# Means of v copied by engines instead of DMAs, and the first up products in parts by head group

## The chip, the cores and the metric

The kernel runs on one core of one Trainium2 chip. The metric is the device time of one execution in microseconds; each kernel is run several times and the median counts. A profile is one more execution, with its own time.

## The reference

Four batches, eight heads, 768 positions, head dimension 64. Each query attends to the keys less than 16 positions away and, beside them, to one summary for each block of 32 keys: the maximum of the block's keys, and the mean of its values. Then a feed-forward layer follows, whose activation is h cos h.

```python
k_sum = k.reshape(B, H, nb, block, D).max(axis=3)
v_sum = v.reshape(B, H, nb, block, D).mean(axis=3)
scores_l = np.where(mask_l, scale * q @ k.T, -1e9)       # |i - j| < 16
scores_s = scale * q @ k_sum.T + np.log(block)
a = softmax(concat(scores_l, scores_s))
x = (a @ concat(v, v_sum)) -> (3072, 512)
h = x @ w_in            # 512 x 2048
out = (h * np.cos(h)) @ w_out
```

(The `@` forms are shortened here; the softmax adds 1e-9 to its sum.) The weights come as 64-bit floats.

## The kernel before, in words

The 3072 rows are eight blocks of 384, two to a batch. In each block the eight heads make four groups of two, `a` to `d`; `a0` is the first group of block 0, `c1` the third of block 1. One group's attention gives 128 of the 512 rows of x, transposed: `x_high` rounds the product to the short float that PE multiplies at full rate, `x_low` takes what is left. x of groups a and b lies in one tile, x of c and d in another.

The layer runs in *steps*: one step takes 128 of the 2048 columns of `w_in` for one block. `up` is 12 matmuls (four groups, three products of high and low parts) into one PSUM bank; `turns` (ACT), `residue` (DVE), `sine` (ACT) and `gate` (DVE) make h cos h; `high_part` and `low_part` split it; `down` and `down_low` are 9 matmuls into three accumulators. Steps s0 to s5 are block 0 with the first six weight slices, s6 to s21 block 1 with all 16, s22 to s31 block 0 with the rest; from s32 on a block is done at a time. A weight slice (`w0` to `w15`) is loaded as raw bytes into one of a few slots and made into floats by `apart` and `first_bits` (ACT), `join` (DVE), and split by `high_part` and `low_part`, the last on DVE or POOL.

Blocks 0 and 1 are done ahead of the layer's first step or beside it. A group there goes: load q and k; transpose k (`tk`, two halves) and q (`tq`) on PE into PSUM; copy them to SBUF (`ck` on ACT or DVE, `cq`); block maxima of k (`ks`, DVE); mask and score matmuls (`ms`, `sc`, PE); minimum (`mx`, DVE), exponentials (`ex`, ACT, six instructions), sums (`sm`, DVE), inverse (`iv`), multiplication (`nm`, POOL); transposes of the weights (`tp`, two pieces, PE), their copies to SBUF (`cp`); the products with the values (`va`, 24 matmuls, PE); `xh` and `xl`.

The value tile of a group has 96 rows of values and, in rows 96 to 119, the 24 block means, the same for each of its six windows. For batch 0 the means are made on PE: `Summaries.load` brings v in two halves (`v0_0.l`, `v0_1.l`, two DMAs each), `Summaries.products` (`vm`, L908) multiplies each by a matrix of 1/32 and 0, `ones`, into 24 rows of a bank; `place` (`ve`, L919) copies four pieces of that bank to four small tiles `means` with ACT; and `load_vs` (`m`, L502) lets SP send each piece to a value tile, six times over, once for each block: eight DMAs in all. The other batches have another way, which stays.

The order is written out by hand: `ORDER` (L32) is one list of tokens such as `a0.tk.1.0`, what to do, with its PSUM banks and its engine (`a`, `v`, `p` for ACT, DVE, POOL). The program walks it, and each engine's queue, SP's too, has its instructions in the order of the list. `FILL` (L22) puts filling matmuls ahead of some tokens (L960): they multiply zeros, and nothing reads them. There are 56 in twelve places.

## Time and profile before

| | us |
|---|---|
| runs shown: median (lowest to highest) | 635.62 (633.67 to 638.09) |
| profiled execution, from its first instruction to its last | 633.6 |
| PE busy in it | 620.6 (98%) |
| DVE, ACT, POOL busy | 426.8, 315.7, 208.7 |
| mean granted clock of TensorE | 1.000 |

The page lists for each engine what share of the span it was busy, then the same in 40 slices of 15.8 us as digits of tenths, and the costliest groups of instructions: line, engine, operation, tiles, shapes and count, then busy us and the mean ns of one, then the idle time of the engine ahead of them and what ended it. The other views used are: busy time of each engine by stretches of the span; the timeline, a row for each run of equal instructions with its start and length; the chain of work that ended last, in order of time; the view of waits. PEld is PE's loading of the stationary operand; SPq the queue from which the DMAs are issued. A matmul's row has its whole length, through which the next ones already run, so the time that one takes of PE is read from many in a row.

### The profile page before, as it was taken

Reading aid. Unit: us, or ns where it says so; the run is one execution under the profiler, and the core shown is the slowest. Engines: PE = TensorE matmul, PEld = TensorE weight load, DVE = VectorE, ACT = ScalarE, POOL = GpSimd, SP = SyncE. Lnnn points to the kernel's source line nnn. Section 1 sums busy time; section 2 is a strip of 40 time slices with the busy share of each in tenths; the row PEclk is TensorE's granted clock in tenths of the full one; section 3 lists DMA queues with packets and bytes.
Section 4 is the critical chain, followed back from the end, with each engine's and each line's share of the span. In section 5 each row is a group of like instructions: output and inputs, shape, how many; then the busy total and the mean of one; then the engine's idle time right before and its main releaser. Section 6 shows DMA issues by size and latency. Waiting matters only on the chain.

```text
span 633.6 us, 12128 instructions
## 1 busy us (share of the span) xinstructions
PE 620.6 (98%) x4596; PEld 546.6 (86%) x4596; DVE 426.8 (67%) x795; ACT 315.7 (50%) x557; POOL 208.7 (33%) x243
## 2 busy tenths in 40 slices
PE   7889999999999999999999999999999999999997
PEld 5469898988889989897998989898888998989895
DVE  5689889986767877766766576657775555554524
ACT  3588776765544454464534554353554352522323
POOL 3136543563532523243434432211432241201000
PEclk9999999999999999999999999999999999999999
DMA  8987876734354465434343544232242313300001
GB/s 218 289 235 203 283 238 187 164 80 109 104 157 123 100 152 117 110 87 115 77 128 98 134 109 109 72 78 62 72 116 87 100 47 98 93 25 34 17 1 50
DMA packets 171305, 74.10 MB, mean 117 GB/s; under 512 B 136944, under 2 KB 160112, under 8 KB 171248
## 3 DMA queue, kind: packets, MB, share of 16 engines
q1 hardware_dynamic: 171104, 73.21, 43.6%
q8 instruction: 36, 0.59, 0.4%
q14 instruction: 21, 0.17, 0.1%
q10 hardware_dynamic: 144, 0.13, 0.1%
HBM read 54.43 MB, written 16.52 MB: 112 GB/s over the span
## 4 chain that ended last, share of the span: by engine, by line
PE 91%; SPq 3%; DVE 2%; DMA 2%; ACT 1%; POOL 0%; issue 0%; DVEq 0%; ACTq 0%
PE banks L738 41%; PE banks L789 41%; PE banks L694 4%; PE banks L581 3%; DMA late<-in_moe_w_out_dram 2%; SPq L468 2%; PE banks L650 1%; PE banks L593 0%; ACT L756 0%; SPq L497 0%; SPq L906 0%; SPq L489 0%; ACT t L756 0%; DVE t L760 0%; DVE xl L389 0%
## 5 line engine op out<-in xcount | busy, mean ns | idle before, releaser
L738 PE MATMUL banks<-xh,w 128*128 128x384 f32 x1024 | 267.0, 337 | 0.0
L789 PE MATMUL banks<-w,gh 128*128 128x512 f32 x768 | 197.4, 392 | 0.6 <-DVE stage L827 0.6
L738 PEld LDWEIGHTS banks<-xh,w 128*128 128x128 f32 x1024 | 185.3, 188 | 2.4 <-issue 1.3
L738 PE MATMUL banks<-xl,w 128*128 128x384 f32 x512 | 171.1, 334 | 0.0
L789 PEld LDWEIGHTS banks<-w,gh 128*128 128x128 f32 x768 | 142.7, 188 | 31.4 <-issue 1.2
L389 POOL TENSOR_TENSOR gl<-t,gh 128x384 fp32r<-128x384 f32 x67 | 68.7, 1029 | 240.2 <-DVE gh L385 84.6
L748 ACT ACTIVATE t<-banks 128x384 int32<-128x384 f32 x128 | 62.3, 489 | 162.4 <-PE banks L738 88.0
L751 DVE SCALAR_TENSOR_TENSOR t<-t,banks 128x384 f32<-128x384 int32 x128 | 69.7, 547 | 66.7 <-ACT t L748 66.3
L789 PE MATMUL banks<-w,gl 128*128 128x512 f32 x384 | 108.7, 391 | 0.0
L760 DVE TENSOR_TENSOR t<-t,banks 128x384 f32<-128x384 f32 x128 | 69.6, 548 | 41.9 <-ACT t L756 40.2
L756 ACT ACTIVATE t<-t 128x384 f32<-128x384 f32 x128 | 66.3, 523 | 63.0 <-DVE t L751 62.7
L738 PEld LDWEIGHTS banks<-xl,w 128*128 128x128 f32 x512 | 96.1, 188 | 0.3
L789 PEld LDWEIGHTS banks<-w,gl 128*128 128x128 f32 x384 | 71.8, 188 | 15.3 <-issue 0.2
L641 POOL TENSOR_TENSOR sc<-sc,r 128x720 f32<-128x720 f32 x28 | 40.1, 1432 | 58.6 <-DVE r L638 54.5
L383 ACT CAST gh<-t 128x384 fp32r<-128x384 f32 x62 | 31.4, 510 | 35.3 <-DVE t L760 19.2
L617 POOL TENSOR_TENSOR sc<-sc,m 128x720 f32<-128x720 f32 x24 | 34.0, 1415 | 44.5 <-DVE m L614 41.3
L389 DVE TENSOR_TENSOR gl<-t,gh 128x384 fp32r<-128x384 f32 x61 | 38.9, 640 | 11.5 <-ACT gh L383 6.6
L385 DVE CAST gh<-t 128x384 fp32r<-128x384 f32 x66 | 25.3, 383 | 15.8 <-PE banks L789 12.5
L254 POOL TENSOR_TENSOR kn<-kn 96x256 f32<-96x256 f32 (+1 forms) x38 | 25.7, 677 | 23.7 <-DMA kn<-in_v_dram 22.0
L601 DVE SCALAR_TENSOR_TENSOR sc<-banks,mask 128x360 f32<-128x360 f32 x48 | 24.2, 519 | 13.4 <-PE banks L581 13.4
L635 DVE TENSOR_REDUCE r<-sc 128x6 f32<-128x726 f32 x28 | 25.1, 897 | 10.0 <-ACT sc L631 9.6
L664 DVE STREAM_TRANSPOSE stage<-sc 128x768 f32<-128x768 f32 x24 | 23.3, 970 | 10.5 <-POOL sc L641 10.2
(115 smaller groups left out, 558.0 us busy)
## 6 DMA issues: line engine op xcount, KB each, us to landing
pd<-stage SPq DMA_DIRECT2D x24, 384.0 KB
late<-in_moe_w_out_dram SPq DMA_DIRECT2D x16, 511.6 KB
late<-in_moe_w_in_dram SPq DMA_DIRECT2D x16, 510.5 KB
pt<-pd SPq DMA_DIRECT2D x72, 96.0 KB
vn<-in_v_dram SPq DMA_DIRECT2D x50, 120.0 KB
out_dram<-stage SPq DMA_DIRECT2D x23, 256.0 KB
kn<-in_v_dram SPq DMA_DIRECT2D x24, 192.0 KB
qn<-in_q_dram SPq DMA_DIRECT2D x96, 48.0 KB
```

The costliest lines, as they stand in the source:

```text
L254: eng.tensor_tensor(out=t[:, :n], in0=t[:, :n], in1=t[:, n:], op=ALU.add)
L383: eng.copy(out=out, in_=in_)
L389: eng.tensor_tensor(out=lo, in0=src, in1=hi.bitcast(F32), op=ALU.subtract)
L617: nc.gpsimd.tensor_tensor(out=self.sc, in0=self.sc, in1=self.m.unsqueeze(2).broadcast_to([P, U, NK]), op=ALU.subtract)
L641: nc.gpsimd.tensor_tensor(out=self.sc, in0=self.sc, in1=self.r.unsqueeze(2).broadcast_to([P, U, NK]), op=ALU.mult)
L694: nc.tensor.matmul(out=self.xps[rows, t * QT : (t + 1) * QT], lhsT=self.vn[:, t, rows], rhs=self.pt[2 * c + hh][s], start=True, stop=True,)
L738: nc.tensor.matmul(out=self.h, lhsT=w_of(name, self.f)[:, c * P : (c + 1) * P], rhs=x_of(self.blk, part, c), start=n == 0, stop=n == last,)
L748: nc.scalar.activation(out=self.t.bitcast(I32), in_=self.h, func=AF.Copy, scale=1.0 / TWO_PI, bias=0.25)
L751: nc.vector.scalar_tensor_tensor(out=self.t, in0=self.t.bitcast(I32), scalar=-TWO_PI, in1=self.h, op0=ALU.mult, op1=ALU.add)
L756: nc.scalar.activation(out=self.t, in_=self.t, func=AF.Sin, scale=-1.0, bias=-0.5 * math.pi)
L760: nc.vector.tensor_tensor(out=self.t, in0=self.t, in1=self.h, op=ALU.mult)
L789: nc.tensor.matmul(out=self.acc[i], lhsT=g[:, i * P : (i + 1) * P], rhs=w_of(name, self.f), start=self.first and n == 0, stop=self.last an ...
```

## The change

Three things.

1. `means` and `place` go. `ones` becomes wider, so that the products of v write 120 rows of the bank, the means in rows 96 to 119 and zeros above. `load_vs` for batch 0 is now an engine's copy of 24 rows and 768 columns: for block 0 from the bank (each piece read six times over), for block 1 from the value tile of the same group of block 0. The engines are ACT for a0, b0, c0, c1; DVE for d0, d1; POOL for a1, b1.
2. `up` is now made of four `up_part`, one for each head group, three matmuls each; a token `pu` calls one alone, and the first to come has the bank. Steps s0 to s5 use it; all later steps call `up` as before, with the same matmuls in the same order.
3. `ORDER` is new from its start up to `s31.tu`; the remaining two thirds of the list, 1396 tokens of 2096, are the old ones. `FILL` keeps one entry, 15 filling matmuls ahead of the first mask (`c0.ms`, now the first token); the other 41 go. In the new part many tokens have another engine: of the high parts of x of blocks 0 and 1, seven of eight are on DVE (all eight were on ACT), the low parts of w1, w0, w4, w7, w6 and w12 went from DVE to POOL and that of w5 from POOL to DVE, and the high parts of w1, w5 and w4 from DVE to ACT.

```diff
-FILL = {"a0.tk.1": 15, "a0.tk.0": 2, "b0.tq": 8, "c0.tk.0": 2, "b0.tk.0": 2, "d0.tk.0": 2, "b0.tk.1": 3, "c0.tp.0": 9, "b1.ms": 4, "b1.tq": 3, "a1.ms": 3, "a0.va": 3}
+FILL = {"c0.ms": 15}
...
-    ones = early[:, U * P : U * P + QC * 3 * HB].rearrange("p (c n) -> p c n", c=QC)
+    ones = early[:, U * P : U * P + QC * (NK + HB)].rearrange("p (c n) -> p c n", c=QC)
...
-        def load_vs(self):
+        def load_vs(self, eng=None):
             if not self.b:
-                nc.sync.dma_start(
-                    out=self.vn[W:NK], in_=means[self.pr].unsqueeze(1).broadcast_to([NB, U, P])
-                )
+                if self.half:
+                    means = groups[0][self.pr].vn[W:NK]
+                else:
+                    means = Summaries.bank[W:NK, self.pr * P : (self.pr + 1) * P].unsqueeze(1).broadcast_to([NB, U, P])
+                copy(eng, self.vn[W:NK], means)
                 return
...
         def up(self, i):
-            self.h = bank(i)[:, :TB]
-            n, last = 0, 3 * NC - 1
             for c in range(NC):
-                for name, part in (("wi_h", 0), ("wi_h", 1), ("wi_l", 0)):
-                    nc.tensor.matmul(
-                        out=self.h, lhsT=w_of(name, self.f)[:, c * P : (c + 1) * P],
-                        rhs=x_of(self.blk, part, c),
-                        start=n == 0, stop=n == last,
-                    )
-                    n += 1
+                self.up_part(c, *([] if c else [i]))
+
+        def up_part(self, c, *i):
+            if i:
+                self.h, self.n = bank(*i)[:, :TB], 0
+            for name, part in (("wi_h", 0), ("wi_h", 1), ("wi_l", 0)):
+                nc.tensor.matmul(
+                    out=self.h, lhsT=w_of(name, self.f)[:, c * P : (c + 1) * P], rhs=x_of(self.blk, part, c),
+                    start=self.n == 0, stop=self.n == 3 * NC - 1,
+                )
+                self.n += 1
...
-                Summaries.bank = bank(*i)[:NB, : H * D]
+                Summaries.bank = bank(*i)[:NK, : H * D]
...
-                    out=Summaries.bank, lhsT=ones[:, c, (1 - self.n) * HB : (3 - self.n) * HB], rhs=t[:, :, c],
+                    out=Summaries.bank, lhsT=ones[:, c, (1 - self.n) * HB :][:, :NK], rhs=t[:, :, c],
...
-        def place(self, eng):
-            for i in range(NG):
-                copy(eng, means[i], Summaries.bank[:, i * P : (i + 1) * P])
```

What the list does to the queues is seen at three places. First PE, at the place where the layer begins. Before (`pt` are the transposed weights of the attention, `early` the value tile of b0, `w_394` the slice w1):

```order
L694 MATMUL banks<-pt,early 64x64 x12
L650 MATMUL banks<-ident,sc 120x128 x6
L738 MATMUL banks<-xh_0_568,w_394 128x384
L738 MATMUL banks<-xl_0_604,w_394 128x384
L738 MATMUL banks<-xh_0_568,w_394 128x384 x2
L738 MATMUL banks<-xl_0_604,w_394 128x384
L738 MATMUL banks<-xh_0_568,w_394 128x384
L738 MATMUL banks<-xh_0_589,w_394 128x384
```

Now (`x_1_156` and `early` are the value tiles of d0 and b0, `w_500` the slice w0, `w_380` w1; `xh_0_597` is x of c and d, `xh_0_527` x of a and b):

```order
L699 MATMUL banks<-pt,x_1_156 64x64 x12
L655 MATMUL banks<-ident,sc 120x128 x4
L747 MATMUL banks<-xh_0_527,w_500 128x384
L747 MATMUL banks<-xl_0_535,w_500 128x384
L747 MATMUL banks<-xh_0_527,w_500 128x384
L747 MATMUL banks<-xh_0_597,w_500 128x384
L747 MATMUL banks<-xl_0_602,w_500 128x384
L747 MATMUL banks<-xh_0_597,w_500 128x384
L699 MATMUL banks<-pt,early 64x64 x12
L524 MATMUL banks<-ident,qn 128x128 x3
```

Before, all values of block 0 stand ahead of the first up product; now two parts of s1 are done behind the values of a0 and c0, and six more of s1 and s0 between the values of d0, of b0 and the scores of d1. The scores of d1 stood ahead of the first up product and now stand behind eight parts.

Second ACT, where the means are copied. Before (`late2` to `late5` hold the small tiles, `stage1` is a raw slice):

```order
L626 ACTIVATE late5_145<-banks_153,m_368 128x120 x6
L383 COPY pt_388<-banks_153 120x256
L383 COPY late2_142<-banks_153 24x128
L383 COPY late3_143<-banks_153 24x128
L383 COPY late4_144<-banks_153 24x128
L383 COPY late5_145<-banks_153 24x128
L417 ACTIVATE stage1_449<-late6_146 128x1024
```

Now (`early`, `vn` and `x1_0` are the value tiles of b0, a0 and c0):

```order
L631 ACTIVATE sc_122<-banks_153,m_360 128x120 x6
L386 CAST w1_380<-stage1_344 128x1024
L386 COPY early_148<-banks_153 24x768
L386 COPY vn_120<-banks_153 24x768
L386 COPY x1_0_155<-banks_153 24x768
L386 COPY pt_398<-banks_153 120x256
L386 COPY kd3_119<-banks_153 128x384 x2
L420 ACTIVATE stage1_480<-late6_146 128x1024
```

Three copies of 768 columns stand in the place of four of 128, ahead of the P^T copies and of d0's k copies.

Third SP's queue of loads, up to the second half of v (`late_140` and `late_141`). Before (`kn` is d0's k):

```order
L468 DMA kn<-in_k_dram 128x6x64 x2
L468 DMA late_142<-in_k_dram 128x6x64 x2
L906 DMA late_140<-in_v_dram 128x4x192 x2
L468 DMA late_145<-in_q_dram 128x3x64 x2
L468 DMA qn<-in_q_dram 128x3x64 x2
L404 DMA late_147<-in_moe_w_in_dram 128x4x1021
L408 DMA late_147<-in_moe_w_out_dram 128x4093
L906 DMA late_141<-in_v_dram 128x4x192 x2
```

Now:

```order
L407 DMA late_147<-in_moe_w_in_dram 128x4x1021
L411 DMA late_147<-in_moe_w_out_dram 128x4093
L471 DMA late_144<-in_q_dram 128x3x64 x2
L471 DMA qn<-in_q_dram 128x3x64 x2
L913 DMA late_140<-in_v_dram 128x4x192 x2
L913 DMA late_141<-in_v_dram 128x4x192 x2
L471 DMA kn<-in_k_dram 128x6x64 x2
```

The slice w1 stands ahead of both halves of v, the halves follow each other, and d0's k comes behind them; the eight DMAs of the means, of 72 KB each, no longer stand further down.

More of the change, by code (lines that the diff above doesn't have):

```diff
@@ L170 @@
+s127.ta.0.0.v s127.st.0 s127.ta.1.1.a s127.st.1 s127.ta.2.a s127.st.2 s127.sb.2
 """
@@ L353, in tile_kernel @@
     HB = NB // 2
-    ones = early[:, U * P : U * P + QC * 3 * HB].rearrange("p (c n) -> p c n", c=QC)
+    ones = early[:, U * P : U * P + QC * (NK + HB)].rearrange("p (c n) -> p c n", c=QC)
     nc.gpsimd.memset(ones, 0.0)
-    nc.gpsimd.memset(ones[:, :, HB : 2 * HB], 1.0 / BLOCK)
+    picks = ones[:, :, W + HB : NK]
+    nc.gpsimd.memset(picks, 1.0 / BLOCK)
     for base, sign in ((0, 1), (BLOCK - 1, -1)):
         nc.gpsimd.affine_select(
-            out=ones[:, :, HB : 2 * HB], in_=ones[:, :, HB : 2 * HB], pattern=[[sign, QC], [-sign * BLOCK, HB]],
+            out=picks, in_=picks, pattern=[[sign, QC], [-sign * BLOCK, HB]],
             compare_op=ALU.is_ge, fill=0.0, base=base, channel_multiplier=sign * QC,
@@ L871, in tile_kernel @@
     vn_b = [carve(late[3 + i // 2], i % 2 * n_v, NK, U, P) for i in range(NG)]
-    means = [carve(late[2 + i], 2 * n_v + TB, NB, P) for i in range(NG)]
     slices = [Slice(f, late[int(i)][:, :RAW]) for f, i in enumerate(SLOTS)]
@@ L940, in tile_kernel @@
         ),
-        Summaries: dict(l="load", h="halve", s="sum", vm="products", ve="place"),
+        Summaries: dict(l="load", h="halve", s="sum", vm="products"),
         Slice: dict(
@@ L946, in tile_kernel @@
         Step: dict(
-            up="up", tu="turns", re="residue", si="sine", ga="gate", hi="high_part",
+            up="up", pu="up_part", tu="turns", re="residue", si="sine", ga="gate", hi="high_part",
             lo="low_part", dh="down", dl="down_low", fe="fetch", ad="add", ta="take", st="store",
```

275 lines of the change are left out of this document (138 added, 137 removed).

## The prediction

> **What bounds the kernel now.** I read the page first: span, busy shares and the row of slices.
>
> ```profile
> span 633.6 us, 12128 instructions
> PE 620.6 (98%) x4596; PEld 546.6 (86%) x4596; DVE 426.8 (67%) x795; ACT 315.7 (50%) x557; POOL 208.7 (33%) x243
> PE   7889999999999999999999999999999999999997
> ```
>
> PE is busy for 98% of the span, and only the first three slices and the last one fall short of 9. The question is thus how much PE time is open, and where. The view of busy time by stretches tells it (PE, PEld, DVE, ACT, POOL, then granted clock, DMA share and GB/s):
>
> ```profile
> 0.00:47.50 47.50, 39.57 (x643) 27.96 (x643) 33.87 (x72) 28.62 (x71) 13.33 (x42) 1.00 0.91 247
> 47.50:160.00 112.50, 112.50 (x740) 101.58 (x739) 96.44 (x159) 76.21 (x128) 56.83 (x57) 1.00 0.64 181
> 160.00:163.00 3.00, 2.38 (x13) 1.97 (x12) 2.47 (x3) 1.63 (x3) 0.91 (x1) 1.00 0.41 134
> 163.00:600.00 437.00, 436.92 (x3063) 389.17 (x3063) 282.32 (x541) 199.81 (x338) 135.62 (x142) 1.00 0.37 93
> ```
>
> From 47.5 to 600 us PE is idle 0.7 us in all. Before 47.5 it is idle 7.9 us, and part of its busy time there is the filling matmuls of L960, which compute nothing. What stands at 47.5 is in the timeline and the chain: the first up product, and behind it four in a row.
>
> ```profile
> 47.50 0.42 PE L738 MATMUL banks<-xh,w 128*128 128x384 f32 x1
> 47.74 8.35 PE banks L738 x48
> ```
>
> So an up matmul takes 8.35/48 = 0.174 us of PE, and from the first one to the end PE is the bound. **A gain can only come from useful matmuls done before 47.5 us; a loss can come from anywhere, since behind 47.5 every wait of PE adds to the span.** The order is new up to step 31; behind that it is the old one, so I let that part run its old length.
>
> **The change, part by part.** I sum against the profiled execution, 633.6 us; the median of the three runs shown, 635.62, lies 2.0 above it, and the forecast is that sum plus 2.0.
>
> *The means.* Before, the second half of v landed late enough to hold PE; ACT then wrote four small tiles, and SP sent them to the value tiles by DMA, the last of the four only at 38.57.
>
> ```profile
> 23.42 2.73 PE L914 MATMUL banks<-late,early 128*24 128x512 f32 x6 [1.21 <-DMA late<-in_v_dram]
> 26.19 0.73 ACT L383 COPY late<-banks 24x128 f32<-24x128 f32 x4 [3.26 <-PE banks L914]
> 38.57 0.82 SPq L504 DMA_DIRECT2D early<-late  x1
> ```
>
> In the new order d0's k (two DMAs) stands behind both halves of v on SP; all other loads ahead of them are the same ones. Its size, by the rows of DMA issues:
>
> ```profile
> kn<-in_k_dram SPq DMA_DIRECT2D x2, 192.0 KB
> ```
>
> That is 0.39 MB, at the 247 GB/s of the first stretch 1.6 us. The second half of v then lands at 21.8 instead of 23.4, and its products end at 24.5. They write 120 rows instead of 24, with as many columns, so I leave them 2.73. ACT now stands still at the first mean copy (b0's) until 24.5; queued behind it are every P^T copy, k copy and score exponential of the first stretch, so **ACT's list from there is the next chain**. No copy of 24x768 is in the trace; the two sizes of ACT's P^T copy give its slope:
>
> ```profile
> L383 ACT COPY pt<-banks 120x512 f32<-120x512 f32 x4 | 2.4, 590 | 0.3 <-PE banks L650 0.2
> L383 ACT COPY pt<-banks 120x256 f32<-120x256 f32 x6 | 2.3, 382 | 1.2 <-PE banks L694 0.7 <-PE banks L650 0.5
> ```
>
> 208 ns for 256 columns makes 0.80 us for 768. The four small copies above took 0.18 us for 128 columns each, so 1.1 for six of them is the upper end; the slope alone, without the 0.17 us that an instruction of this line costs beside it, is the lower, 0.6. For the two copies on POOL the nearest rows are the clearing of a tile's edge and a subtraction:
>
> ```profile
> L877 POOL MEMSET x<- 120x128 f32 x2 | 0.3, 203 | 0.0
> L389 POOL TENSOR_TENSOR gl<-t,gh 128x384 fp32r<-128x384 f32 x67 | 68.7, 1029 | 240.2 <-DVE gh L385 84.6 <-PE banks L789 66.7 <-ACT gh L383 65.0
> ```
>
> 0.2 us, and twice 1.03 for 768 columns: between 0.2 and 2.1, middle 1.1, and hidden, since POOL is idle for over two thirds of the first stretch.
>
> *ACT's list up to the first up product's turns.* The other durations:
>
> ```profile
> L417 ACT ACTIVATE stage<-late 128x1024 f32<-128x1024 int8 x16 | 18.4, 1151 | 6.0 <-DMA late<-in_moe_w_out_dram 4.0 <-DVE w L389 1.7 <-POOL w L389 0.3
> L422 ACT ACTIVATE stage<-stage 128x1024 int32<-128x1024 f32 x16 | 16.9, 1059 | 0.3
> 29.99 1.60 ACT L626 ACTIVATE sc<-banks,m 128x120 f32<-128x120 f32 x6
> L383 ACT COPY kd<-banks 128x384 f32<-128x384 f32 x6 | 2.8, 480 | 4.6 <-PE banks L532 4.6
> L525 ACT ACTIVATE qd<-banks 128x384 f32<-128x384 f32 x2 | 1.0, 502 | 2.3 <-PE banks L519 2.3
> L383 ACT CAST w<-stage 128x1024 fp32r<-128x1024 f32 x4 | 4.2, 1047 | 1.1 <-DVE stage L429 1.1
> ```
>
> Between the wait and the first turns (`s0.tu`) the new order gives ACT: 4 mean copies 3.2; 2 k copies 0.96; 4 short and 2 long P^T copies 2.7; `apart` and `first_bits` of w0, w2, w5 6.63; 4 sets of exponentials 6.4; 3 q copies 1.5; one w cast 1.05. Sum 22.4, with 26 gaps of 0.03 us between neighbours 23.2. From 24.5 that ends at 47.7, and the q copy of d1, 0.8 us earlier, at 46.9. d1's scores follow on PE (1.0 us): **48.0 us for what PE had behind it at 47.5 before.** But by then 8 up parts (of s1 and s0), 24 matmuls, are done as well, in the gaps: 24 x 0.174 = 4.2 us. DVE comes out about even: four casts of x and a mean copy go to it, two slice casts and, net, one slice low part leave it. **Term 1: 4.2 - 0.5 = 3.7 us won.** The removed fillings are worth nothing in themselves, they lay in waits.
>
> *The next 14 us.* Further rows:
>
> ```profile
> L748 ACT ACTIVATE t<-banks 128x384 int32<-128x384 f32 x128 | 62.3, 489 | 162.4 <-PE banks L738 88.0 <-DVE gl L389 35.8 <-POOL gl L389 34.6
> L756 ACT ACTIVATE t<-t 128x384 f32<-128x384 f32 x128 | 66.3, 523 | 63.0 <-DVE t L751 62.7
> L756 ACT ACT_TABLE_LOAD x23 | 29.5, 1283 | 0.4
> L383 ACT CAST gh<-t 128x384 fp32r<-128x384 f32 x62 | 31.4, 510 | 35.3 <-DVE t L760 19.2 <-PE banks L789 14.8 <-DVE t L751 1.2
> L383 ACT CAST xh<-banks 128x384 fp32r<-128x384 f32 x23 | 10.9, 481 | 11.1 <-PE banks L694 11.1
> 36.74 0.85 PE banks L694 x24
> 37.59 0.58 PE banks L650 x4
> 93.48 8.20 PE banks L789 x36
> ```
>
> From 48.0 PE has 12 more parts (6.3 us, steps 2, 5 and 3), one set of values 0.85, one of P^T 0.58 and the down products of s0 and s1 (18 x 8.20/36 = 4.1): it reaches the down product of s2 at 59.8. That one needs s2's gate cast on ACT. ACT's list from 47.7 to there: 4 turns 2.0, 3 sines 1.6, the table load 1.3, `apart` and `first_bits` of w3 and w4 4.4, exponentials 1.6, w4's cast 1.05, two P^T copies 0.97, an x cast 0.48 and the gate cast 0.51: 13.9, with 17 gaps 14.4, so 62.1. **Term 2: PE waits 2.3 us there.** If ACT is not that late at 47.7, it is 0; if v lands as late as before, 3.9. Late next is the last x part of block 1 (DVE), for the first step of that block: one cast and one low part, some 1.1 us, if the wait ahead did not cover it; it does, so 0.
>
> *Steps 6 to 31.* Same work, newly ordered; before, PE waited 0.6 us there. I take no change; 0.6 less is one end, 2 us more (the same as term 2 once again) the other.
>
> Sum: 3.7 - 2.3 = 1.4 won, 632.2 us of the execution and **634.2 us** as a median. Its own range, from 0.3 and 3.9 for term 2, 0.6 less and 2 more behind, and 0.6 to 1.1 for a copy: 631 to 638.5.
>
> **The rivals.**
>
> *Full cover: the waits of term 2 do not come.* For it: PE never waits in the row of 47.50:160.00, though DVE is busy 86% there. Against: that had no up matmul done ahead. Then 3.7 to 4.3 us are won: 629.3 of the execution at best, 631.3 to 632 as a median.
>
> *POOL slows DVE, and the kernel gets slower.* Place: 25 to 79 us, where w1, w0, w4 and w9 now have their low parts on POOL (one slice before), with two mean copies: 3 x 2.49 + 2 x 1.1 = 9.7 us more POOL work. The rows: the same join, beside a normalisation on POOL and alone.
>
> ```profile
> 34.86 1.39 POOL L641 TENSOR_TENSOR late<-late,r 128x720 f32<-128x720 f32 x1 [7.32 <-DVE r L638]
> 35.65 1.69 DVE L429 SCALAR_TENSOR_TENSOR stage<-late,stage 128x1024 int32<-128x1024 int32 x1
> 41.73 1.22 DVE L429 SCALAR_TENSOR_TENSOR stage<-late,stage 128x1024 int32<-128x1024 int32 x1
> L389 POOL TENSOR_TENSOR w<-stage,w 128x1024 fp32r<-128x1024 f32 x6 | 14.9, 2490 | 20.0 <-DVE w L385 10.6 <-ACT w L383 7.5 <-DMA qn<-in_q_dram 1.9
> 47.50:60.00 12.50, 12.50 (x95) 12.22 (x94) 12.11 (x16) 10.58 (x22) 7.49 (x5) 1.00 0.74 195
> 60.00:70.00 10.00, 10.00 (x71) 8.39 (x70) 7.80 (x17) 7.45 (x15) 7.48 (x11) 1.00 0.95 286
> 70.00:79.00 9.00, 9.00 (x83) 7.26 (x82) 8.42 (x14) 6.31 (x12) 3.09 (x3) 1.00 0.77 261
> ```
>
> 0.6 us of overlap cost the join 0.47, so 0.78 of it. If half of the new POOL time meets such an instruction, DVE loses 3.8 us. It decides from 3.2 us on, DVE's idle time from 47.5 to 79 (31.5 less 28.3); past that point the delay comes on top of term 2 whole, since the lists are late there already: 632.2 + 3.8 = 636.0, as a median 638.0, slower than before by 0.4%. [...]
>
> *The clock falls.* The fillings between 5 and 47 us go, and with them the activity that stands in PE's waits.
>
> ```profile
> L960 PE MATMUL banks<-part_sum 128*128 128x256 bf16 x56 | 9.7, 312 | 2.8 <-ACT sc L626 1.1 <-DVE part_sum L279 1.1 <-ACT kd L383 0.6
> ```
>
> And from the view of waits, PE alone, its longest:
>
> ```profile
> PE banks L914 <- DMA late<-in_v_dram: 1.2, 1, 1.2
> ```
>
> Before, no idle stretch is longer than 1.2 us, and the granted clock is 1.00 in every stretch above. In the new order I find 2.3 us between the q transposes and the scores of c0, near 12 us. At half clock the two products of v would take 2 x 2.73 more at worst, one of them behind the landing, so ACT's list starts 2.7 later: 634.9, as a median 636.9. [...]
>
> *The parts fill no gap*, because their x comes as late as in the old order: then the 8 parts run behind 48.0, term 1 is -0.5, and with term 2 covered by their 4.2 us the time is 634.1, as a median 636.1.
>
> **How the numbers follow.** The forecast has a chance of 0.45, full cover 0.25, POOL against DVE 0.15, the clock 0.08, no gap filled 0.07. The measurement tells about 1% of this kernel, 6.4 us, from no change. Under 629.3 lies only the far end of full cover, 0.09; over 642 only contention that goes on behind 79 us, 0.08; 0.83 is left between. The range takes in full cover with v landing 2.3 us earlier still (629) and contention that meets five sixths of POOL's new time instead of half (6.3 us, 640.5).
>
> **What would show it.** Right: the first up matmul before 37 us, d1's scores ending near 48, ACT's first three mean copies done by 28, an idle stretch of PE of about 2 us near 60 that an ACT cast ends, and nothing new behind 90. The join near 1.2 us and the clock at 1.00 would put two rivals away. Wrong: no idle PE from 48 to 80 (term 2), scores of d1 ending at 50 or later (term 1), or PE idle over 2 us between 80 and 190.

## The result, and the profile after

The changed kernel takes **644.97 us** (median of 4 runs, 643.82 to 646.80) against 635.23 for the kernel before on the same chip; the ratio is 1.0145, with a 95% interval of 1.0111 to 1.0179. It is slower, by 9.7 us. The prediction said 634.2, within 629 to 640.5, and no change. Three executions of the runs below took 762 to 1228 us; the medians leave them out.

The page of the changed kernel, its profiled execution (line numbers behind the edits have moved: up products are now L747, down products L797, ACT's copies L386, DVE's and POOL's L388, low parts L392):

```profile
span 644.1 us, 12036 instructions
PE 622.7 (97%) x4555; PEld 544.8 (85%) x4555; DVE 438.3 (68%) x806; ACT 314.6 (49%) x547; POOL 215.0 (33%) x244
PEclk9999999989999999999999999999999999999999
```

DVE is busy 11.5 us longer than before, ACT 1.1 us less; and one slice of the clock, the ninth (129 to 145 us), is no longer full. The stretches, as in the prediction but cut at 78 us, where block 1's first up product now begins (PE, PEld, DVE, ACT, POOL, then granted clock, DMA share and GB/s):

```profile
0.00:47.50 47.50, 38.35 (x574) 27.93 (x575) 36.29 (x76) 30.86 (x72) 19.76 (x46) 1.00 0.95 253
47.50:78.00 30.50, 29.66 (x271) 24.86 (x271) 26.98 (x45) 22.50 (x40) 17.90 (x17) 1.00 0.61 182
78.00:160.00 82.00, 75.24 (x399) 64.62 (x398) 68.00 (x101) 46.73 (x70) 36.03 (x31) 0.98 0.53 145
...
163.00:600.00 437.00, 436.69 (x3106) 389.41 (x3106) 287.93 (x549) 200.25 (x338) 138.21 (x148) 1.00 0.38 97
```

PE is idle 0.8 us from 47.5 to 78 and 0.3 us behind 163. **From 78 to 160 it is idle 6.8 us, where the kernel before was never idle.** The weights of block 1's first up product are loaded at 77.6 us (before: 78.5), those of the program's last up matmul at 624.9 (before: 614.4): up to step 5 the changed kernel is 0.9 us ahead, which is less than executions of one and the same start differ by (shown below the table of runs), and behind it it loses 11.5. PE's waits in that stretch, by what ended them (us in total, times, longest):

```profile
PE banks L797 <- DVE gh L388: 2.8, 4, 1.2
PE banks L797 <- DVE gl L392: 1.8, 2, 1.0
PE banks L586 <- ACT t L764: 1.4, 1, 1.4
PE banks L797 <- POOL gl L392: 0.3, 1, 0.3
PE banks L747 <- DVE xh L388: 0.3, 1, 0.3
PE banks L747 <- DVE xl L392: 0.2, 1, 0.2
```

Down products wait for the two parts of a gate, gh and gl, which DVE writes. Why DVE is late stands in its groups for 78 to 160 us, first of the changed kernel, then of the kernel before (count, busy us, mean ns of one):

```profile
L392 DVE TENSOR_TENSOR gl<-t,gh 128x384 fp32r<-128x384 f32 x10 | 10.1, 1011 | 1.1 <-DVE gh L388 0.5
L388 DVE CAST gh<-t 128x384 fp32r<-128x384 f32 x14 | 9.8, 708 | 0.6
L759 DVE SCALAR_TENSOR_TENSOR t<-t,banks 128x384 f32<-128x384 int32 x17 | 9.2, 541 | 5.0 <-ACT t L756 5.0
```

```profile
L751 DVE SCALAR_TENSOR_TENSOR t<-t,banks 128x384 f32<-128x384 int32 x19 | 10.2, 545 | 4.5 <-ACT t L748 4.4
L389 DVE TENSOR_TENSOR gl<-t,gh 128x384 fp32r<-128x384 f32 x10 | 6.6, 681 | 1.1 <-ACT gh L383 0.8
L385 DVE CAST gh<-t 128x384 fp32r<-128x384 f32 x7 | 2.5, 360 | 0.9 <-PE banks L789 0.4
```

The gate cast stands on DVE twice as often (14 against 7), and one takes 708 ns instead of 360; a low part takes 1011 instead of 681. The residue, one of whose inputs lies in PSUM, keeps its length (541 against 545). Single rows of the timeline show what happens (start, length; DVE and POOL, then PE's wait behind it):

```profile
106.86 2.38 DVE L388 CAST gh<-t 128x384 fp32r<-128x384 f32 x1
109.34 0.56 DVE L392 TENSOR_TENSOR gl<-t,gh 128x384 fp32r<-128x384 f32 x1
...
106.62 2.40 POOL L392 TENSOR_TENSOR w<-stage,w 128x1024 fp32r<-128x1024 f32 x1 [2.55 <-PE banks L747]
...
109.29 0.97 PE L797 MATMUL banks<-w,gh 128*128 128x512 f32 x3 [0.58 <-DVE gh L388]
```

A cast that takes 0.36 us elsewhere starts 0.24 us after POOL's low part of slice 12, takes 2.38, and ends 0.22 us after that has ended: **it was done only behind POOL's instruction.** The same happens at 84.5 us (1.66) and 97.0 (a low part, 2.31 in place of 0.56), with the low parts of slices 7 and 6 on POOL, and at 147.4 (2.55) with that of slice 15. The order shows why this is new: among slices 6 to 15 POOL has the low parts of 6, 7, 10, 12, 14 and 15 where it had 10, 13, 14 and 15 (that of slice 9 it has in both), and of the gates of steps 6 to 18 DVE casts 12 and ACT 1, where it was 6 and 7.

### The profile page after: what moved, and what is told of

It is laid out like the page before. It is cut to its first block, busy times and chain, and to the rows that moved or that the text cites. A ratio compares the mean times of both kernels' runs of the same rounds, so it can differ in the third digit from the quotient of the medians.

```text
span 644.1 us, 12036 instructions
## 1 busy us (share of the span) xinstructions
PE 622.7 (97%) x4555; PEld 544.8 (85%) x4555; DVE 438.3 (68%) x806; ACT 314.6 (49%) x547; POOL 215.0 (33%) x244
## 4 chain that ended last, share of the span: by engine, by line
PE 76%; DVE 8%; DMA 7%; issue 2%; ACT 2%; SPq 2%; POOL 2%; DVEq 0%; POOLq 0%; ACTq 0%
PE banks L797 35%; PE banks L747 34%; PE banks L699 3%; PE banks L586 3%; DMA kn<-in_v_dram 2%; DVE stage L432 2%; DMA x<-in_v_dram 1%; DVE gh L388 1%; DVE gl L392 1%; POOL kn L256 1%; DMA part_d<-late 1%; PE banks L921 1%; DMA kn<-in_k_dram 1%; DMA late<-in_moe_w_out_dram 1%; SPq L465 1%
## 5 line engine op out<-in xcount | busy, mean ns | idle before, releaser
L747 PE MATMUL banks<-xh,w 128*128 128x384 f32 x1024 | 271.6, 339 | 0.7 <-POOL w L392 0.4
L797 PE MATMUL banks<-w,gh 128*128 128x512 f32 x768 | 198.2, 393 | 3.5 <-DVE gh L388 3.1
L747 PEld LDWEIGHTS banks<-xh,w 128*128 128x128 f32 x1024 | 186.5, 189 | 4.5 <-issue 1.3
L797 PEld LDWEIGHTS banks<-w,gh 128*128 128x128 f32 x768 | 142.4, 188 | 36.0 <-DVE gh L388 5.8
L747 PE MATMUL banks<-xl,w 128*128 128x384 f32 x512 | 172.2, 336 | 0.4 <-DVE xl L392 0.4
L392 POOL TENSOR_TENSOR gl<-t,gh 128x384 fp32r<-128x384 f32 x62 | 65.7, 1063 | 256.7 <-DVE gh L388 104.8
L797 PE MATMUL banks<-w,gl 128*128 128x512 f32 x384 | 109.4, 393 | 2.1 <-DVE gl L392 1.8
L747 PEld LDWEIGHTS banks<-xl,w 128*128 128x128 f32 x512 | 96.7, 189 | 1.8 <-DVE xl L392 1.1
L797 PEld LDWEIGHTS banks<-w,gl 128*128 128x128 f32 x384 | 71.3, 188 | 18.2 <-DVE gl L392 2.6
L392 DVE TENSOR_TENSOR gl<-t,gh 128x384 fp32r<-128x384 f32 x66 | 45.9, 697 | 12.3 <-ACT gh L386 6.4
L388 DVE CAST gh<-t 128x384 fp32r<-128x384 f32 x76 | 34.5, 455 | 14.8 <-PE banks L797 11.2
L386 ACT CAST gh<-t 128x384 fp32r<-128x384 f32 x52 | 26.4, 510 | 30.1 <-DVE t L768 18.2
```

Of the source, the lines that this page charges most:

```text
L386: eng.copy(out=out, in_=in_)
L388: eng.tensor_copy(out=out, in_=in_)
L392: eng.tensor_tensor(out=lo, in0=src, in1=hi.bitcast(F32), op=ALU.subtract)
L747: nc.tensor.matmul(out=self.h, lhsT=w_of(name, self.f)[:, c * P : (c + 1) * P], rhs=x_of(self.blk, part, c), start=self.n == 0, stop=self. ...
L797: nc.tensor.matmul(out=self.acc[i], lhsT=g[:, i * P : (i + 1) * P], rhs=w_of(name, self.f), start=self.first and n == 0, stop=self.last an ...
```

## The experiments

Each median is of 4 to 12 executions. The last two columns are from the one profiled execution of each: when the weights of block 1's first up product are loaded, and how long it is from there to those of the last up matmul.

| run | median us | before, same chip | ratio (95%) | block 1 begins | from there |
|---|---|---|---|---|---|
| before | | | 1 | 78.5 | 535.9 |
| changed kernel | 644.97 | 635.23 | 1.0145 (1.0111 to 1.0179) | 77.6 | 547.4 |
| new start, old rest | 639.67 | 634.85 | 1.0078 (1.0052 to 1.0103) | 78.4 | 540.1 |
| old start, new rest | 650.72 | 634.56 | 1.0241 (1.0214 to 1.0267) | 81.3 | 545.2 |
| only the means by copies | 642.11 | 634.56 | 1.0116 (1.0089 to 1.0144) | 86.4 | 538.8 |
| old order, four low parts on POOL | 642.57 | 634.85 | 1.0121 (1.0082 to 1.0159) | 76.1 | 545.2 |
| six low parts on DVE | 644.40 | 634.85 | 1.0132 (1.0090 to 1.0175) | 80.3 | 547.0 |
| four casts on ACT | 645.78 | 635.67 | 1.0161 (1.0137 to 1.0186) | 78.4 | 547.4 |
| with fillings | 643.72 | 635.67 | 1.0127 (1.0104 to 1.0151) | 77.7 | 545.1 |
| five low parts on DVE, fillings | 639.97 | 634.68 | 1.0079 (1.0052 to 1.0106) | 77.1 | 540.7 |
| five low parts as ACT casts, fillings | 638.33 | 634.39 | 1.0067 (1.0044 to 1.0089) | 77.0 | 539.9 |
| b2's q turn earlier | 646.25 | 634.85 | 1.0174 (1.0137 to 1.0212) | 77.4 | 546.9 |
| fillings near 130 us | 644.45 | 634.68 | 1.0140 (1.0113 to 1.0167) | 78.2 | 545.5 |
| new start mended, old rest | 635.64 | 635.67 | 1.0000 (0.9986 to 1.0013) | 76.4 | 539.8 |
| two ups later | 635.67 | 634.68 | 1.0015 (0.9995 to 1.0034) | 75.8 | 539.4 |
| slice 8 behind the sines | 635.99 | 634.56 | 1.0025 (1.0007 to 1.0043) | 75.6 | 538.8 |
| hybrid with less on DVE | 636.31 | 634.39 | 1.0017 (0.9997 to 1.0036) | 75.4 | 540.0 |
| two waits more mended | 635.40 | 634.68 | 1.0008 (0.9992 to 1.0023) | 76.5 | 538.0 |

The column "block 1 begins" varies by itself. The run with four low parts on POOL has the old list, letter for letter, up to the low part of slice 7, and yet it reaches block 1 at 76.1 us, where the profile of the kernel before has 78.5. In it the second half of v had landed when PE came to it (before: 1.21 us of wait), and the first up matmul stands at 45.16 us instead of 47.50:

```profile
45.16 0.42 PE L737 MATMUL banks<-xh,w 128*128 128x384 f32 x1
```

So a difference of some 2 us in that column does not tell two starts apart.

### Which part of the new order

**New start, old rest.**

```diff
 s5.dl s5.ta.0.a s5.st.0
-s7.up.3 s7.tu s7.re w7.hi.a s5.ta.1.a s5.st.1 s5.ta.2.a s7.si s6.up.5 s7.ga s7.hi.v
+s6.up.2 w7.hi.v w8.ab.0 s6.tu s6.re s7.up.3 s7.tu s7.re s6.si w8.sh s7.si w7.lo.v s7.ga s6.ga
...
```

> The changed order up to the first store of step 5, then the order of before for everything that is left: the same work, engine letters included, as before from step 6 on. Theory (the loss lies in the new order of steps 6 to 31, where POOL's low parts of the slices hold up DVE's casts beside them): the new start brings the first product of block 1 at 77.8 us instead of 78.7, and PE waits under 1 us between 80 and 160, so 634.3 us, between 633.0 and 636.5. Rival (the new start leaves the lists of DVE and ACT late, and the waits of 80 to 160 us are its echo): 640 to 645 us, with 4 us or more of PE waits in that stretch.

It gave 639.67 us, between the two and nearer to the rival. Half of the loss is gone (1.0078 against 1.0145), but the start does not carry over free of cost. PE's waits from 78 to 160 us, and two stretches of the start with the clock:

```profile
PE banks L745 <- DVE t L766: 2.7, 1, 2.7
...
24.55:27.96 3.41, 0.84 (x38) 0.70 (x41) 2.87 (x5) 2.73 (x5) 2.55 (x3) 1.00 1.07 189
27.96:31.37 3.41, 3.41 (x76) 2.73 (x68) 1.40 (x4) 1.08 (x2) 0.00 (x0) 0.50 1.10 335
```

The up product of step 10 stood 2.65 us for its bank, which a gate on DVE sets free, and the clock fell to 0.50 at 28 us, right behind the 2.57 us wait of a1's scores. So about half of the loss lies in the new order behind step 5, as my theory had it, and about half comes with the new start, as the rival had it.

**Old start, new rest.** Here the old order, with its fillings and whole up products, has the means by engine copies, and the changed order begins behind the join of slice 7.

```diff
 b1.xh.a s5.dh s5.lo.v s5.dl w6.l v1_3.s.v c1.xl v1_4.l b1.xl d1.xl w9.lo.p w7.ab.1 w7.sh w7.fb
-s6.up.2 w7.hi.v s5.ta.0.a w8.ab.0 s6.tu s6.re s7.up.3 s7.tu
+a2.q v1_4.s.p v1_5.l w12.l s5.ta.0.a s5.st.0 s7.up.3 s7.tu s7.re w7.hi.a s5.ta.1.a
...
```

> The order of before, its fillings and whole up products, with the means by engine copies, up to the join of slice 7; behind it the changed order of what is left, POOL's low parts of slices 6, 7, 10, 12, 14 and 15 among it. Theory (the rest is what costs, whatever the start): as in the changed kernel DVE's casts and low parts stand beside POOL's 2.4 us instructions, PE waits 6 us or more between 80 and 160 us and the clock falls at least once there: 643 us, between 640.5 and 646. Rival (the lateness comes from the new start): the waits shrink under 2 us, 636 to 638 us.

650.72 us, above what either expected, since the start is slow by itself (next run); the profiled execution is the fastest of the six, and no fall of the clock lies in its rest. But from block 1's first product on it takes 545.2 us, 9.3 more than before and close to the changed kernel's 547.4, with the same waits:

```profile
PE banks L794 <- DVE gh L385: 3.4, 5, 1.3
PE banks L583 <- ACT t L761: 1.4, 1, 1.4
```

So the loss of the rest does not come from the new start.

**Only the means by copies.**

```diff
-v0_0.vm.4 v0_1.l v0_1.vm v0_1.ve.a
+v0_0.vm.4 v0_1.l v0_1.vm b0.m.a a0.m.a c0.m.a d0.m.v
...
-b0.m
...
-d0.m
```

> The order of before with one edit of the change alone: the products of v give 120 rows, and engine copies write the means into the value tiles (b0, a0 and c0 on ACT and d0 on DVE right behind the products, the second halves on POOL, ACT and DVE) in place of four small ACT copies and the DMAs. Theory (the named edits are harmless, the loss is made behind step 5): ACT's list gets 3 x 0.80 - 0.73 = 1.7 us longer ahead of the first up product, and PE waits nowhere else: 636.5 us, between 635 and 638. Rival (the copies themselves, or what they hold up, make the loss): 640 us and more.

642.11 us: the rival. The first up product comes at 53.7 instead of 47.5 us,

```profile
53.71 0.48 PE L744 MATMUL banks<-xh,w 128*128 128x384 f32 x1
...
48.00:54.00 6.00, 4.45 (x80) 4.18 (x80) 2.43 (x6) 3.25 (x12) 0.95 (x1) 0.72 0.69 148
```

because ACT and DVE now both stand for v's landing, with everything queued behind; the granted clock is lower as well, a mean of 0.72 from 48 to 54 us. The edit that I had taken as small is paid for by the lists behind it, and the new start is what makes up for that: with it block 1 begins at 77.6 us, not at 86.4.

### POOL beside DVE

**Old order, four low parts on POOL.**

```diff
-w7.lo.v
+w7.lo.p
-w6.lo.v
+w6.lo.p
-w8.lo.v
+w8.lo.p
-w12.lo.v
+w12.lo.p
```

> The kernel of before, its own order, with the low parts of slices 6, 7, 8 and 12 on POOL instead of DVE: four letters. DVE has 4 x 1.22 = 4.9 us less to do, POOL 4 x 2.4 = 9.6 us more, between 80 and 110 us, where before had no PE wait. Theory (POOL's instruction stalls DVE's casts and two-input operations beside it): DVE instructions of 1.3 us and more appear there that took 0.35 to 0.7, PE waits 1 to 4 us, 636 to 640 us. Rival (POOL harmless): DVE is only relieved, no PE wait, 635.2 us within 0.7.

642.57 us, 7.7 more, though DVE was relieved of 4.9 us. Four letters make four fifths of the changed kernel's loss, without any other part of the change. One pair of rows, DVE and POOL, and PE's waits from 78 to 160 us:

```profile
96.76 2.84 DVE L388 TENSOR_TENSOR gl<-t,gh 128x384 fp32r<-128x384 f32 x1
...
96.80 2.38 POOL L388 TENSOR_TENSOR w<-stage,w 128x1024 fp32r<-128x1024 f32 x1
...
PE banks L788 <- DVE gh L384: 3.0, 1, 3.0
PE banks L737 <- DVE t L759: 2.4, 2, 1.6
```

The low part of a gate, 0.55 us elsewhere, took 2.84 beside POOL's, and every queue position behind it was late. The clock fell as well, to a mean of 0.60 from 116 to 120 us.

**Six low parts on DVE.**

```diff
-w7.lo.p w6.lo.p w12.lo.p w10.lo.p w14.lo.p w15.lo.p
+w7.lo.v w6.lo.v w12.lo.v w10.lo.v w14.lo.v w15.lo.v
```

> The changed kernel with the low parts of slices 6, 7, 10, 12, 14 and 15 on DVE instead of POOL, nothing else. Theory (POOL's 2.4 us instructions stall DVE): the DVE instructions that took 1.2 to 2.6 us in place of 0.35 to 1.2 between 84 and 150 us fall back, some 9 us of stalls against 6 x 1.22 = 7.3 us of new DVE work, so 641 to 644 us, and no gate cast over 0.7 us there. Rival A (DVE simply has too much work, POOL is harmless): PE waits up to 7 us more, 648 to 652 us. Rival B (the products stand in a worse order, the engines do not matter): 645 us as the changed kernel.

644.40 us (641.14 to 648.29): no clear answer. The stalls went, but a low part on DVE now held an up product by 2.9 us, and the clock fell three times, twice ahead of 36 us (means of 0.55 and 0.59 from 12 to 20 us, 0.69 and 0.89 from 28 to 36, 0.50 from 116 to 120); the runs' mean clock went from 0.987 (648.29 us) to 0.999 (641.14).

**Four casts on ACT.**

```diff
-s7.hi.v s11.hi.v w13.hi.v s18.hi.v
+s7.hi.a s11.hi.a w13.hi.a s18.hi.a
```

> The changed kernel with four casts on ACT instead of DVE: the gates' high parts of steps 7, 11 and 18 and that of slice 13, all of which took 0.7 to 2.0 us longer beside a POOL instruction than elsewhere. POOL's work stays. Theory (POOL holds up DVE's SBUF-to-SBUF casts, and ACT's are free of it): the casts take their 0.51 and 1.05 us on ACT, DVE is relieved of about 5.9 us, of which the low parts behind them, still beside POOL, take 1 to 2 back: 641 us, between 639 and 643. Rival A (ACT's casts are held up as well): they take over 1 us on ACT, 645 us. Rival B (DVE's lateness has other causes): 644 to 646 us with ordinary durations.

645.78 us, rival B's number but not its reason. On ACT the casts take their 0.51 us; what stands beside POOL now is DVE's next instruction, the low part, which takes 1261 ns against 1011 in the changed kernel:

```profile
L390 DVE TENSOR_TENSOR gl<-t,gh 128x384 fp32r<-128x384 f32 x10 | 12.6, 1261 | 3.6 <-ACT gh L384 3.1
```

So here the wait went from one instruction of DVE to the next; the two runs that follow take POOL's instructions away.

**Five low parts on DVE, with fillings** (those of the run with fillings, below).

```diff
-w7.lo.p w6.lo.p w12.lo.p w14.lo.p w15.lo.p
+w7.lo.v w6.lo.v w12.lo.v w14.lo.v w15.lo.v
```

> The changed kernel with the three fillings, and the low parts of slices 6, 7, 12, 14 and 15 on DVE; that of slice 10, beside which no DVE instruction took longer, stays on POOL. With six on DVE the runs at a mean clock of 0.99 and more gave 641 to 644.7, and those of the changed kernel 643.7 with fillings. Theory (POOL's low parts cost 4 us of waits, the missing fillings 1 to 2, and both add): 639.5 us, between 638 and 641. Rival (the two do not add, since one wait is replaced by the next): 642 to 644 us.

639.97 us, as the theory had it. With 6.1 us more work on DVE the rest takes 540.7 us instead of 545.1.

**Five low parts as ACT casts, with fillings.** ACT casts the slice a second time where the low part stood, so this kernel leaves the low parts of five slices out, and its output is not the reference's.

```diff
         def low_part(self, eng):
+            if eng is nc.scalar:
+                copy(eng, wm[self.f][:, 2 * DM :], self.uf)
+                return
             rest(eng, wm[self.f][:, 2 * DM :], self.uf, wm[self.f][:, : 2 * DM])
...
-w7.lo.p w6.lo.p w12.lo.p w14.lo.p w15.lo.p
+w7.lo.a w6.lo.a w12.lo.a w14.lo.a w15.lo.a
```

> The changed kernel with the three fillings; the low parts of slices 6, 7, 12, 14 and 15 are left out as such: ACT casts the slice a second time in their place (1.05 us each), so the output is not the reference's, and neither POOL nor DVE has that work. On POOL the five gave 643.7 us, on DVE 640.2. Theory (POOL's instructions cost by holding up DVE, and on DVE the 6.1 us of work still cost something): 638 us, between 636.5 and 639.5, no DVE gate cast or low part over 1.6 us between 80 and 150. Rival (the order behind step 5 costs whatever DVE and POOL do, by fewer products queued ahead): 640 to 642 us, with PE waits as in the run with five on DVE.

638.33 us, as the theory had it. DVE's two groups have their durations of the kernel before (360 and 681), in the changed kernel's own order:

```profile
L390 DVE TENSOR_TENSOR gl<-t,gh 128x384 fp32r<-128x384 f32 x10 | 6.4, 643 | 0.7
L386 DVE CAST gh<-t 128x384 fp32r<-128x384 f32 x15 | 5.3, 358 | 0.6
...
PE banks L587 <- ACT t L765: 1.4, 1, 1.4
PE banks L798 <- DVE gh L386: 1.0, 1, 1.0
```

By the ratios, the five instructions cost 0.6% of 634.4, 3.8 us (1.0127 less 1.0067); within the profiled executions 5.2 us of the rest. What is left, 539.9, is what the old rest takes behind the new start as well (540.1). So POOL's five instructions cost some 0.6 of the changed kernel's 1.45%; what the gate casts that went from ACT to DVE cost by themselves, no run tells.

### The clock

**With fillings.**

```diff
-FILL = {"c0.ms": 15}
+FILL = {'c0.ms': 15, 'a0.ms': 4, 'c0.sc': 6, 'a1.ms': 9}
```

> The changed kernel with filling matmuls (they compute nothing) put back into three PE waits of the first 28 us: 4 ahead of a0's masks, 6 ahead of c0's scores, 9 ahead of a1's masks. Theory (without fillings the clock falls in the first stretch in some executions, so the mean over runs pays 1 to 2 us for it, and the wait near 130 us keeps its own fall): the runs' mean clock rises from 0.997 to 0.998 or 0.999, 643.5 us, between 642.5 and 644.5, and the profile shows 1.00 up to 130 us. Rival (the first stretch's clock does not matter): 645 us.

643.72 us, the expected size; but its interval overlaps that of the changed kernel, and the runs' mean clock did not rise (0.997 in both). That the fillings are worth 1 us is thus only likely.

**b2's q turn earlier.**

```diff
+b2.qt
 w13.fb w14.l w13.hi.v b2.kw.a a2.mx s15.dh s15.dl w15.ab.1 s17.tu s17.re s18.si s17.si
-b2.qt
 b2.sc.1.2
```

> The changed kernel with one instruction moved: DVE's transposition of b2's q ahead of the join of slice 13, some five DVE instructions earlier. In the changed kernel b2's scores waited 1.44 us at 130.05, and the clock stood at 0.5 from 132.2 to 135.6 us, 1.6 us lost. Theory (that transposition is what the scores waited for, and the clock fell by that wait): both go, 642.0 us, between 641 and 643, clock 1.00 in that stretch. Rival A (the wait goes, the clock falls all the same): 643.5. Rival B (the next wait takes its place): 645 and the clock as before.

646.25 us: rival B. b2's scores no longer wait, but the up product behind them does, 2.21 us, for a gate on DVE, and the clock falls right behind that wait, as it did before:

```profile
131.71 0.44 PE L745 MATMUL banks<-xh,w 128*128 128x384 f32 x1 [2.21 <-DVE t L766]
...
132.00:135.40 3.40, 3.40 (x12) 3.40 (x12) 2.16 (x4) 0.61 (x2) 1.86 (x1) 0.52 0.90 227
```

**Fillings near 130 us.** In that place the fillings multiply the identity's bits, which computes nothing that is used.

```diff
-FILL = {"c0.ms": 15}
+FILL = {'c0.ms': 15, 'b2.sc': 8}
```

> The changed kernel with 8 filling matmuls ahead of b2's scores, where PE waited 1.44 us at 130.05 and the clock stood at 0.5 for 3.4 us behind it; they compute nothing and write the bank that the scores then overwrite. The wait itself stays. Theory (idle time of PE just ahead makes the clock fall, here 0.34 and 1.44 us within 2.8): the clock stays at 1.00 there, the up products behind it come every 0.174 us, 645.0 - 1.6 = 643.4 us, between 642.7 and 644.2. Rival (the clock falls there for another reason, such as heat or load over a longer time): 645 us, and 0.5 as before.

644.45 us, between the two. In the profile the clock stays at 1.00 in that place; first two stretches of the changed kernel, then two of this run (each as long as the fall, 3.41 us):

```profile
128.82:132.23 3.41, 1.70 (x27) 1.13 (x27) 3.21 (x6) 2.24 (x4) 0.22 (x1) 1.00 0.83 273
132.23:135.64 3.41, 3.41 (x16) 3.37 (x12) 2.27 (x4) 1.31 (x2) 1.86 (x1) 0.50 0.55 113
```

```profile
127.34:130.76 3.42, 3.25 (x16) 2.20 (x15) 3.38 (x5) 2.29 (x4) 1.83 (x1) 1.00 0.17 41
130.76:134.17 3.41, 2.88 (x39) 2.42 (x37) 3.21 (x7) 1.47 (x2) 0.98 (x1) 1.00 0.95 305
```

Ahead of the fall PE was busy for 1.70 of 3.41 us, here for 3.25 and 2.88. But without the fillings' own rows it would still be 2.1 in the second stretch, and behind 2.08 of 3.41 us the clock of the changed kernel held at 1.00 (26.42 to 29.83 us, last section). So this execution does not show that the fillings kept it up. The gain in the median is smaller than the 1.7 us that I estimate for one fall (3.41 x 0.5), and not resolved: in this execution the clock fell at 28 us instead (means of 0.59 and 0.56 from 28 to 32 us).

### Can the new start be kept?

These five stand on the new start with the old rest. The first edits the run "new start, old rest", the second and third each the run ahead of it, and the last two both edit "slice 8 behind the sines".

**New start mended, old rest.**

```diff
-FILL = {"c0.ms": 15}
+FILL = {'c0.ms': 15, 'a0.ms': 4, 'c0.sc': 6, 'a1.ms': 9}
...
-d0.m.v a0.cp.0.v d0.ck.1.a c0.nm d0.tk.0.4 d0.ck.0.a a1.cq.v
+a0.cp.0.v d0.ck.1.a c0.nm d0.tk.0.4 d0.ck.0.a a1.cq.v d0.m.v
...
-s10.up.2 s15.up.3 s5.ta.1.a s8.tu s5.ta.2.a s9.tu s9.re s8.re s8.si s11.up.0
+s10.up.2 s5.ta.1.a s8.tu s5.ta.2.a s9.tu s9.re s8.re s8.si s11.up.0 s15.up.3
```

> The new start with the order of before from step 6 on, and three mends. d0's mean copy on DVE goes behind a1's q copy (it stood at 22.7 us and was done at 26.5, and a1's scores waited for the q copy behind it, 2.57 us); the up product of step 15 goes behind that of step 11 (its bank was free 2.65 us late); the fillings of the run with fillings. Theory: both waits go and the clock holds, so 639.7 less 2.65, less 1 to 2 of the first, less 2 of clock: 633.5 us, between 632 and 635.5. Rival (DVE's list behind the new start is late as a whole, so the waits come back at the next product): 637 to 639 us.

635.64 us, level with the kernel before and, by the ratios, 5 us better than unmended; which of the three mends won it, no run tells. The up product that I moved was that of step 15, while the one that had waited was that of step 10. It waits again, 1.93 us at 85 us, with a fall of the clock behind:

```profile
PE banks L746 <- DVE t L767: 1.9, 1, 1.9
...
88.60:91.00 2.40, 2.40 (x9) 2.40 (x8) 2.37 (x4) 2.16 (x5) 0.00 (x0) 0.50 0.94 360
```

**Two ups later.**

```diff
-s10.up.2 s5.ta.1.a s8.tu s5.ta.2.a s9.tu s9.re s8.re s8.si s11.up.0 s15.up.3
+s5.ta.1.a s8.tu s5.ta.2.a s9.tu s9.re s8.re s8.si s11.up.0 s10.up.2 s15.up.3
```

> The mended new start with the old rest, and the up product of step 10 behind that of step 11 as well. In the mended run step 10's up product waited 1.93 us at 85.2 for its bank, which the gate of step 6 set free late, and the clock fell to 0.5 right behind it. Bank 0, for step 11, is free by then, so 2.1 us of products come ahead of it. Theory: the wait and the fall both go, and nothing else changes, 635.64 - 1.93 - 1.7 = 632.0 us, between 631.3 and 633.5. Rival (the down product of step 6 waits instead, since its gate is just as late): 634 to 635.6 us.

635.67 us, just above the rival's range: the wait moved to the down products (0.6 and 0.33 us at 96 and 98) and to the next up product.

**Slice 8 behind the sines.**

```diff
-w8.ab.0 s6.tu s6.re s7.up.3 s7.tu s7.re s6.si w8.sh s7.si w7.lo.v
+s6.tu s6.re s7.up.3 s7.tu s7.re s6.si s7.si w8.ab.0 w8.sh w7.lo.v
```

> The mended new start with the old rest and the two later up products, and on ACT the first two passes of slice 8 behind the turns and sines of steps 6 and 7 instead of ahead of them. In the run with two up products later ACT stood 4.4 us at 77.2 for slice 8's load (to 81.7), the turns of step 6 behind it, and DVE 4.4 us for those; from there DVE ran at 94% until 103 and PE lost 2.8 us between 84 and 104. Theory (the load's late landing at the head of ACT's queue, not the amount of work, makes the lists late): PE's waits of 95 to 104 us go, 635.8 - 2.8 = 633.0 us, between 632 and 634.3. Rival (DVE's work itself is the bound of this stretch): 635 to 636 us.

635.99 us: the rival's time. The waits went from 96 to 102 and 124 us (0.8 and 1.2).

**Hybrid with less on DVE.** The same second casts on ACT in place of the low parts, which are left out, for slices 6, 7, 8, 11 and 12.

```diff
-w7.lo.v w6.lo.v w8.lo.v w12.lo.v w11.lo.v
+w7.lo.a w6.lo.a w8.lo.a w12.lo.a w11.lo.a
```

> The run with slice 8 behind the sines (new start, old rest, 636.0 us), with the low parts of slices 6, 7, 8, 11 and 12 left out as such: ACT casts the slice a second time in their place, so the output is not the reference's; DVE has 6.1 us less to do between 78 and 115 us, ACT 5.3 more. Theory (what the new start wins ahead of 78 us is given back behind it because DVE's lists do not get ahead with PE): PE's waits of 2.0 us and more near 102 and 124 go, 633.3 us, between 632 and 634.7. Rival (loads and the order hold PE there, not DVE): 635.5 to 637 us.

636.31 us: no gain. A wait of 1.49 us came up near 96 us, for a gate cast on ACT, which had got 5.3 us more; so the run does not tell DVE's amount of work from the order.

**Two waits more mended.**

```diff
-s11.si s10.re w12.lo.v w10.sh w10.fb s11.ga
+s11.si s10.re s11.ga w12.lo.v w10.sh w10.fb
...
-a2.sc.2.3 c2.kt.0 a2.z.1.v a2.z.0.v s14.dh s14.dl
+s14.dh s14.dl a2.sc.2.3 c2.kt.0 a2.z.1.v a2.z.0.v
```

> The run with slice 8 behind the sines (636.0 us) and two moves more, at the two PE waits it had left behind step 5: the gate of step 11 goes ahead of the low part of slice 12 and the join of slice 10 on DVE (the up product of step 14 waited 0.79 us at 101.2 for its bank), and the down product of step 14 goes ahead of a2's scores on PE (they waited 1.21 us at 123.0 for the gate of step 16). Theory (each wait is one queue position, and nothing stands right behind it): 636.0 - 0.8 - 1.2 - 0.3 for the pipeline's two restarts = 633.7 us, between 632.7 and 634.7, below the kernel before. Rival (the engines' lists as a whole do not come earlier, so other waits take their place): 635.3 to 636.5 us.

635.40 us: the rival again, with 1.02 us of wait for a gate on DVE at 104.

No version here is faster than the kernel before. PE comes to block 1 at 75.4 to 76.5 us, 2 to 3 us ahead of the profile of before, but level with the old start that came at 76.1; so what the new start wins by itself is not resolved. Behind it PE is held again within 50 us, by gates for the most part. Whether the loads or the lists make these late stays open.

## Why the prediction was wrong

**Term 1, right in kind, too large.** The mean copies took what was worked out, and began 1.2 us earlier than I had them (the first of the three on ACT, then DVE's, and DVE's q copy of a1):

```profile
23.33 0.80 ACT L386 COPY early<-banks 24x768 f32<-24x768 f32 x1 [1.86 <-PE banks L921]
...
25.55 0.96 DVE L388 COPY x<-banks 24x768 f32<-24x768 f32 x1 [2.84 <-ACT x L386]
27.15 0.55 DVE L532 TENSOR_SCALAR qd<-banks 128x384 f32<-128x384 f32 x1
```

I had looked for the next chain on ACT alone. DVE's copy came only after ACT's three, and a1's q copy stood behind it. The rows of PE that I had named as signs, the first up matmul, d1's scores and s2's down product:

```profile
27.75 1.09 PE L598 MATMUL banks<-kd,qd 64*64 64x96 f32 x48 [2.57 <-DVE qd L532]
...
34.43 0.44 PE L747 MATMUL banks<-xh,w 128*128 128x384 f32 x1
...
48.30 1.09 PE L598 MATMUL banks<-kd,late 64*64 64x96 f32 x48
...
61.84 1.45 PE L797 MATMUL banks<-w,gh 128*128 128x512 f32 x5 [0.42 <-ACT gh L386]
```

The first up matmul came at 34.4 (before 37, as said), the 24 up matmuls were done, and d1's scores ended at 49.4 instead of 48.0. In this execution term 1 is so 4.2 - 1.9 = 2.3 us, not 3.7.

**Term 2, too large.** The gate cast on ACT did end a wait near 62 us, but of 0.42 us, with 0.42 more at 65 for slice 4's low part on POOL; I had 2.3. The two errors nearly cancel: block 1 begins 0.9 us earlier, where 3.7 less 2.3 had been 1.4. The x parts of block 1, taken as covered, cost PE 0.5 us (xh and xl in the waits above).

**"Steps 6 to 31. Same work, newly ordered; ... I take no change" is the step that failed.** I allowed 2 us and it was 11.5. The work was not the same: the order's letters move low parts of slices from DVE to POOL and gate casts from ACT to DVE, and I counted letters only up to step 5. The casts and low parts of gates alone are 14 x (708 - 360) and 10 x (1011 - 681) ns, 8.2 us, longer than by the durations of before. PE's waits there sum to 6.8 us and the fall of the clock, by an estimate, to 3.41 x 0.5 = 1.7. Of the last 3 us the rows explain about half: a down product's row has 0.39 us, of which it takes 8.20/36 = 0.23 of PE, so by my estimate the idle time that a row shows is some 0.16 us less than what the wait costs, and there are ten waits. The rest is not broken down. The sign named for this, PE idle over 2 us between 80 and 190, is what came.

**The rival of POOL against DVE had the cause, in the wrong place and at too low a price.** I looked for it between 25 and 79 us and ended its POOL work there. DVE was held there too (a join at 38.05 us took 1.89 in place of 1.22), but PE waited only 0.75 us for DVE behind it (at 43.2, for a P^T copy), and whether that is its echo was not followed. I also took three slices' low parts as new on POOL in that stretch; before, those of w5 (48.74 us) and w9 (74.97) were on it already, so two are new. The sign I had chosen against it, the join of slice 1 near 1.2 us, came true (1.21 us) and proved nothing, since the instructions held up are others. The price, 0.78 of the overlap, came from one join, and its row was misread: 0.47 of 0.60 us is not a share but the whole overlap less 0.13. A longer overlap in the kernel before would have told this, a small addition beside a slice's low part:

```profile
75.80 1.65 DVE L273 TENSOR_TENSOR vs<-vs,part_sum 96x64 f32<-96x64 f32 x1
...
74.97 2.39 POOL L389 TENSOR_TENSOR w<-stage,w 128x1024 fp32r<-128x1024 f32 x1 [4.73 <-ACT w L383]
```

It takes 0.22 us elsewhere, and here 1.65, until 0.09 us after POOL's end: it lost 1.43 of 1.56 us of overlap, again all but 0.13. The cast at 106.86 lost 2.02 of 2.16, all but 0.14. The residue, whose one input lies in PSUM, kept its length: at 96.55 us, wholly beside POOL's low part of slice 6, one took 0.56. Why those rows were held and this one was not, no run shows.

**The clock** did fall, as another rival had it, though in the profiled execution at 132 us and not in the start. In the profiles of other runs with this start it fell at 28 us (with the old rest to 0.50, from 27.96 to 31.37 us), behind the wait of a1's scores.

The median lies 0.9 us above the profiled execution, where 2.0 had been taken. So, to 0.1 us, the error of 10.8 us is the 11.5 of steps 6 to 31, 0.5 of the first two terms together, less 1.1 of that offset.

## What to carry to other kernels

Before a stretch is called the same work, count its instructions by engine, letter by letter, in both orders. Work that went from DVE to POOL was not free here, though POOL was idle for two thirds of the time: beside a POOL instruction of 2.4 us a gate's cast took 2.38 us in place of 0.36, and a gate's low part 2.84 in place of 0.55. So look in the trace for what stands on DVE beside each such instruction, and price it by the whole overlap. Time won ahead of a stretch where PE has no slack was not kept in any of the five last runs; look first whether the engines that feed the stretch come earlier as well. And compare a start with several executions of the old one before calling it earlier.
